# One written list for the attention phase of a windowed-attention and expert-layer kernel

## The chip, the cores and the metric

The kernel runs on one core of a Trainium2 chip. The metric is device time in microseconds (us) of one execution. The engines are named as in the profile: PE (TensorE) multiplies matrices, PEld is its weight load, DVE (VectorE), ACT (ScalarE) and POOL (GpSimd) do the work on elements, SP issues the DMAs. Each engine takes its own instructions strictly in the order in which the program lists them, and waits at the first one whose inputs or buffers are not ready.

## The reference

Three layers in a row, in float32: a causal attention with a window of 64 keys, four ReLU experts weighted by gate probabilities, and a layer with x·cos(x).

```python
scores = scale * np.matmul(q, k.transpose(0, 1, 3, 2))     # 2 batches, 8 heads, 576 rows, 64 wide
scores = np.where((rel >= 0) & (rel < 64), scores, -1e9)
attn = np.exp(scores - scores.max(-1)) ; attn = attn / (attn.sum(-1) + 1e-09)
x = np.matmul(attn, v)                                     # then 1152 rows of 512
p = domain_probs / (domain_probs.sum(-1) + 1e-09)
for e in range(4):
    out += p[:, e:e + 1] * (np.maximum(x @ w1[e], 0.0) @ w2[e])
h = out @ w_in
return (h * np.cos(h)) @ w_out
```

## The kernel before, in words

**Precision.** A float32 product is made of three fast products: each operand is split into a high part and a low part, and high·high, high·low and low·high are summed. Each weight unit (128 x 1024 numbers) is therefore loaded as `raw`, then split: ACT writes `whi` (`split_hi`, L160), POOL subtracts and writes `wlo` (`split_lo`, L168, in two halves for the first 16 units; unit 4 goes to DVE). The activations have `xhi` and `xlo`, the hidden layer `hh` (ACT) and `hl` (DVE).

**Attention** works on 18 blocks of 64 query rows. A block u goes through stages, named by letters in the code: R (POOL or ACT turns q, L219), S (PE scores, for a pair of blocks, L300), M (DVE mask and row maximum, two instructions, L315), E (ACT four exponentials and a row sum, L328), N (DVE reciprocal, then POOL multiplies, L341), T (PE transposes, L348), P (DVE copies, L355), V (PE times v, for a pair, L360) and X (ACT writes `xhi`, DVE `xlo`, for a pair, L377). PE therefore needs results of DVE, ACT, POOL and DVE again between S and V of one pair.

**Experts.** The 1152 rows are cut into three groups: 256 rows (blocks 0 to 3), 384 (blocks 4 to 9) and 512 (blocks 10 to 17). An expert's hidden layer is cut in halves; group g of half-expert e has four A steps (`emit_a`, L456: 12 matmuls into one bank of PSUM, then `hh` and `hl`) and four B steps (`emit_b`, L513, which sums into 2, 3 or 4 banks). Half-experts 0 and 1 run over the three groups first, so that the first group's experts can start while the attention of later blocks still runs. A step of the first group needs `xhi` and `xlo` of blocks 0 to 3, and units 0 to 3 (for e = 0) or 4 to 7 (e = 1).

**What sets the order.** A short list `START` (L616) fixes the order up to the first A step. After that each stage has a due time (`WHEN`, L596), and `between` (L664), which is called after every three matmuls of a step, issues what is due. Weight units are loaded and split by a pace (`weights`, L680, with a few early exceptions in `EARLY`), at the end of steps. `hh`, `hl` and an expert's weighted sums (`finish`, L552) are issued at once when their matmuls have been issued. Small matmuls on a constant (`keep_busy`, L285) fill PE's gaps in START.

**Shared buffers.** Four PSUM banks serve scores, transposes, V's results and the A steps in turn (`bank`, L71); four `raw` buffers serve the weight loads; SP issues all loads in one queue.

Of the kernel before, what the change touches and what calls it, by code (L numbers as in the profile page):

```python
# [24 lines left out]
def tile_window_attention_moe_cosglu(  # L25
# [134 lines left out]
    def split_hi(n):  # L160
        hi = wp.tile(list(raw_t[n].shape), F32R, tag="whi", name="whi")
        nc.scalar.activation(out=hi, in_=raw_t[n], func=AF.Copy)  # L162
        w_hi[units[n]] = hi
# [16 lines left out]
    LO_DVE = (4,)  # L180
    LO_HALF = 16

    EARLY = {3: 1, 4: 4, 5: 0, 6: 2, 7: 9}

    def split_unit(n):
        split_hi(n)
        if n in LO_DVE:
            split_lo(n, nc.vector)
        elif n < LO_HALF:
            split_lo(n, nc.gpsimd, 0)  # L190
            later(0.5, split_lo, n, nc.gpsimd, 1)
        else:
            split_lo(n, nc.gpsimd)
# [106 lines left out]
    def att_s(u):  # L300
        if u % 2:
            return
# [38 lines left out]
    def att_n(u):  # L341
        e, r = e_t.pop(u), sm_t.pop(u)
        ri = smp.tile([P, NP, 1], F32, tag="ri", name="ri")
        nc.vector.reciprocal(out=ri[:, :, 0], in_=r)
        nc.gpsimd.tensor_tensor(out=e, in0=e, in1=ri.to_broadcast([P, NP, 2 * W]), op=ALU.mult)  # L345
        pn_t[u] = e
# [108 lines left out]

    def emit_a(s):  # L456
# [3 lines left out]
        whi, wlo = w_hi[e, 0, u], w_lo[e, 0, u]  # L460
        xh, xl = xhi[g], xlo[g]
        assert all(("X", j | 1) in done for j in range(G0[g] // W, (G0[g] + n) // W))
        ps = bank("ph")[:, :n]
        cs = slice(P * fo, P * (fo + 1))
        for d in range(KD):
            nc.tensor.matmul(out=ps, lhsT=whi[:, d, cs], rhs=xh[:, d, :], start=d == 0, stop=False)  # L466
            nc.tensor.matmul(out=ps, lhsT=whi[:, d, cs], rhs=xl[:, d, :], start=False, stop=False)  # L467
            nc.tensor.matmul(  # L468
                out=ps, lhsT=wlo[:, d, cs], rhs=xh[:, d, :], start=False, stop=d == KD - 1
            )  # L470
            between((d + 1) / KD)
        hh = hp.tile([P, 512], F32R, tag="hh", name="hh")[:, :n]
        hl = hp.tile([P, 512], F32R, tag="hl", name="hl")[:, :n]
        if e < NM:
            nc.scalar.activation(out=hh, in_=ps, func=AF.Relu)  # L475
            nc.vector.scalar_tensor_tensor(  # L476
                out=hl, in0=ps, scalar=0.0, in1=hh.bitcast(F32), op0=ALU.max, op1=ALU.subtract
            )
            h_t[s] = (hh, hl)
        else:  # L480
            cos_stages(s, ps, hh, hl, n)

# [30 lines left out]
    def emit_b(s):  # L513
# [3 lines left out]
        whi, wlo = w_hi[e, 1, u], w_lo[e, 1, u]  # L517
        hh, hl = h_t.pop(s)
        first, last = f == 0, f == NFC - 1
        no = n // P  # L520
        if first:
            b_ps[g] = [psb.tile([P, 512], F32, tag="psb", name="pb_acc") for _ in range(no)]
        for i in range(no):
            ps = b_ps[g][i]
            cs = slice(P * i, P * (i + 1))
            ops = ((hh[:, cs], whi[:, fo, :]), (hh[:, cs], wlo[:, fo, :]), (hl[:, cs], whi[:, fo, :]))
# [24 lines left out]

    def finish(e, g):  # L552
        n = GS[g]
        pss = b_ps.pop(g)
        if e < NM:
# [5 lines left out]
            for i in range(n // P):  # L561
# [3 lines left out]
                if e == 0:  # L565
                    nc.vector.tensor_scalar(out=a, in0=pss[i], scalar1=p, scalar2=None, op0=ALU.mult)
                    continue
                nc.vector.scalar_tensor_tensor(  # L568
                    out=a, in0=pss[i], scalar=p, in1=a, op0=ALU.mult, op1=ALU.add
                )  # L570
# [20 lines left out]
    stage = {  # L591
        "S": att_s, "M": att_m, "E": att_e, "N": att_n, "T": att_t, "P": att_p, "V": att_v,
        "X": att_x, "R": att_r,
    }

    WHEN = dict(zip("SMENTPVX", (0.0, 0.21, 1.07, 1.09, 1.94, 2.07, 2.55, 2.73)))  # L596
    DEPTH = 3.1
    done = set()

    def att(what, j, *args):  # L600
        if 0 <= j < NB and (what, j) not in done:
            done.add((what, j))
# [12 lines left out]

    START = (  # L616
# [3 lines left out]
    )  # L620
    loads = {"q": load_q, "k": load_k, "v": load_v, "u": load_unit, "D": load_unit}
# [3 lines left out]
    for x in START.split():  # L625
        what, j = x[0], int(x[1:] or 0)
        if what in loads:
            loads[what](j)
        elif what == "g":
            load_gate()  # L630
        elif what == "Y":
            gate_t()
        elif what == "G":
            gate()
        elif what == "H":
            split_hi(j)
        elif what == "L":
            split_lo(j, nc.gpsimd, 0)
        elif what == "l":
            split_lo(j, nc.gpsimd, 1)  # L640
        elif what == "W":
            keep_busy(j)
        elif what.islower():
            att(what.upper(), j, nc.scalar.copy)
        else:
            att(what, j)
    make_mask((1,))
    R0 = GS[0] // W
    flat = sorted(
        (r - R0 + at, what, r)  # L650
        for r in range(R0, NB) for what, at in (*WHEN.items(), ("R", -0.9 - r % 2))
        if (what, r) not in done
    )
    pos = [0]


    def side_upto(x):
        while pos[0] < len(flat) and flat[pos[0]][0] <= x:
            att(*flat[pos[0]][1:])
            pos[0] += 1  # L660

    X0, X1, X2 = -1.0, GS[1] // W + DEPTH - 0.3, NB - R0 + DEPTH

    def between(part):  # L664
# [15 lines left out]
    def weights(t):  # L680
        n = nsplit[0]
        if t < EARLY.get(n, paced[0] + PACE):
# [13 lines left out]
    T1, T2 = SPL * TV - 2, 2 * SPL * TV - 2  # L696
# [9 lines left out]
    for t, (what, s) in enumerate(seq):  # L706
# [10 lines left out]
        if t == T2:  # L717
            side_upto(X2)
            assert pos[0] == len(flat)
# [44 lines left out]
```

## Time and profile before

| | |
|---|---|
| median of 3 runs | 661.45 us (661.2 to 662.39) |
| the profiled execution | 661.49 us |
| its span in the trace | 659.7 us |
| PE busy | 645.8 us, 98% |
| DVE, ACT, POOL busy | 377.5, 272.8, 152.4 us |
| mean granted clock of TensorE | 0.995 |

The profile is of one execution. Its first two parts say how long each engine was busy and in which fortieth of the span; the chain of work says what the last instruction waited for, step by step. A busy PE is not PE at its peak: its matmuls overlap and at a lower granted clock each takes longer. So the useful views here are those of a stretch: its windows (busy time and clock), and the instructions in order of time with the idle time ahead of each.

### The profile page before, as it was taken

How to read it: one execution, taken by the hardware profiler on the slowest of the kernel's cores; microseconds unless marked ns; L12 is line 12 of the kernel's file. 1: busy time of each engine (PE TensorE's matmuls, PEld its weight loads, DVE VectorE, ACT ScalarE, POOL GpSimd, SP SyncE). 2: the span in 40 equal slices, each digit the busy share in tenths (PEclk: the TensorE clock that was granted, in tenths of full speed). 3: DMA queues.
4: the chain of work that ended last, by engine and by line, in shares of the span. 5: the costliest groups of instructions: out<-in, count | busy, mean ns of one | idle time of the engine just before them, and what ended most of it. 6: DMA issues, size and time to landing. Idle time of an engine off the chain costs nothing.

```text
span 659.7 us, 9438 instructions
## 1 busy us (share of the span) xinstructions
PE 645.8 (98%) x3766; PEld 560.0 (85%) x3766; DVE 377.5 (57%) x563; ACT 272.8 (41%) x578; POOL 152.4 (23%) x117
## 2 busy tenths in 40 slices
PE   7889999999999999999999999999999999999997
PEld 6778888888899888899888899888988899988896
DVE  4466642174679566579665668834434355443554
ACT  6656531122123121113121112126876868865664
POOL 4864310231334021113121114012102202200000
PEclk9989999999999999999999999999999999999999
DMA  9565205105324621334342134231102100000022
GB/s 287 201 201 161 65 1 192 33 0 192 142 78 172 215 93 67 127 129 154 134 159 92 68 128 160 88 103 40 58 0 65 64 1 1 1 0 1 0 65 80
DMA packets 34686, 63.02 MB, mean 96 GB/s; under 512 B 2249, under 2 KB 18121, under 8 KB 34642
## 3 DMA queue, kind: packets, MB, share of 16 engines
q1 hardware_dynamic: 34642, 62.42, 28.0%
q8 instruction: 29, 0.48, 0.3%
q14 instruction: 15, 0.12, 0.1%
HBM read 51.66 MB, written 10.75 MB: 95 GB/s over the span
## 4 chain that ended last, share of the span: by engine, by line
PE 93%; POOL 2%; ACT 2%; DVE 1%; DMA 1%; issue 0%; SPq 0%; DVEq 0%; POOLq 0%; ACTq 0%
PE pb_acc L528 44%; PE ph L466 15%; PE ph L468 15%; PE ph L467 15%; PE psv L369 1%; POOL wlo L175 1%; PE pss L309 1%; PE pst L352 1%; POOL e L345 1%; PE psx L540 1%; DMA qraw<-in_q_dram 1%; ACT e L333 0%; PE idle_ps L287 0%; DVE nm L325 0%; ACT whi L162 0%
## 5 line engine op out<-in xcount | busy, mean ns | idle before, releaser
L175 POOL TENSOR_TENSOR wlo<-raw,whi 128x1024 fp32r<-128x1024 f32 (+1 forms) x62 | 121.6, 1972 | 372.9 <-ACT whi L162 283.6
L466 PE MATMUL ph<-xhi,whi 128*128 128x256 f32 (+2 forms) x576 | 195.4, 339 | 0.0
L467 PE MATMUL ph<-xlo,whi 128*128 128x256 f32 (+2 forms) x576 | 193.8, 336 | 0.1
L468 PE MATMUL ph<-xhi,wlo 128*128 128x256 f32 (+2 forms) x576 | 193.8, 336 | 0.0
L528 PE MATMUL pb_acc<-whi,hh 128*128 128x512 f32 x432 | 170.7, 395 | 0.3 <-ACT hh L502 0.3
L528 PE MATMUL pb_acc<-wlo,hh 128*128 128x512 f32 x432 | 169.8, 393 | 0.0
L528 PE MATMUL pb_acc<-whi,hl 128*128 128x512 f32 x432 | 169.3, 392 | 0.0
L475 ACT ACTIVATE hh<-ph 128x256 fp32r<-128x256 f32 (+2 forms) x96 | 47.0, 491 | 286.0 <-PE ph L468 283.0
L476 DVE SCALAR_TENSOR_TENSOR hl<-ph,hh 128x256 fp32r<-128x256 f32 (+2 forms) x96 | 52.9, 554 | 128.3 <-ACT hh L475 128.2
L466 PEld LDWEIGHTS ph<-xhi,whi 128*128 128x128 f32 x576 | 109.1, 189 | 10.9 <-issue 0.5
L467 PEld LDWEIGHTS ph<-xlo,whi 128*128 128x128 f32 x576 | 109.1, 189 | 10.3 <-DVE xlo L387 0.3
L468 PEld LDWEIGHTS ph<-xhi,wlo 128*128 128x128 f32 x576 | 109.0, 189 | 7.5
L528 PEld LDWEIGHTS pb_acc<-whi,hl 128*128 128x128 f32 x432 | 81.5, 189 | 17.6 <-DVE hl L505 0.2
L528 PEld LDWEIGHTS pb_acc<-whi,hh 128*128 128x128 f32 x432 | 81.8, 189 | 16.4 <-issue 0.8
L528 PEld LDWEIGHTS pb_acc<-wlo,hh 128*128 128x128 f32 x432 | 81.7, 189 | 14.4
L490 DVE SCALAR_TENSOR_TENSOR r<-kk,ph 128x256 f32<-128x256 f32 (+2 forms) x48 | 26.6, 555 | 64.5 <-ACT kk L489 64.5
L162 ACT ACTIVATE whi<-raw 128x1024 fp32r<-128x1024 f32 x48 | 50.6, 1054 | 2.1 <-DMA raw<-in_moe_w_dram 2.1
L488 ACT ACTIVATE kk<-ph,bias_m 128x256 f32<-128x256 f32 (+2 forms) x48 | 27.9, 581 | 39.5 <-PE ph L468 39.3
L568 DVE SCALAR_TENSOR_TENSOR acc<-pb_acc,gate_p,acc 128x512 f32<-128x512 f32 x63 | 43.2, 741 | 0.0
L499 DVE TENSOR_TENSOR ph<-ph,r 128x256 f32<-128x256 f32 (+2 forms) x48 | 27.0, 562 | 27.6 <-ACT r L496 27.6
L505 DVE TENSOR_TENSOR hl<-ph,hh 128x256 fp32r<-128x256 f32 (+2 forms) x48 | 26.6, 555 | 16.7 <-ACT hh L502 16.7
L333 ACT ACTIVATE e<-s,nm 128x128 f32<-128x128 f32 x72 | 27.9, 390 | 13.5 <-DVE nm L325 13.5
(65 smaller groups left out, 484.6 us busy)
## 6 DMA issues: line engine op xcount, KB each, us to landing
raw<-in_moe_w_dram SPq DMA_DIRECT2D x32, 512.0 KB, 6.1
raw<-in_moe_w_in_dram SPq DMA_DIRECT2D x8, 1024.0 KB, 6.9
w<-r SPq DMA_DIRECT2D x16, 512.0 KB, 3.1
raw<-in_moe_w_out_dram SPq DMA_DIRECT2D x8, 1024.0 KB, 6.9
raw<-w SPq DMA_DIRECT2D x16, 512.0 KB, 4.0
vr<-in_v_dram SPq DMA_DIRECT2D x16, 256.0 KB, 4.1
qraw<-in_q_dram SPq DMA_DIRECT2D x18, 128.0 KB, 4.4
out_dram<-acc SPq DMA_DIRECT2D x18, 128.0 KB, 1.8
```

Source lines behind the costliest of these rows:

```text
L162: nc.scalar.activation(out=hi, in_=raw_t[n], func=AF.Copy)
L175: engine.tensor_tensor(out=lo[:, cs], in0=t[:, cs], in1=hi[:, cs], op=ALU.subtract)
L333: nc.scalar.activation(out=e[:, p], in_=s[:, p], func=AF.Exp, bias=nm[:, p:p + 1], scale=1.0, accum_out=sm[:, p:p + 1],)
L466: nc.tensor.matmul(out=ps, lhsT=whi[:, d, cs], rhs=xh[:, d, :], start=d == 0, stop=False)
L467: nc.tensor.matmul(out=ps, lhsT=whi[:, d, cs], rhs=xl[:, d, :], start=False, stop=False)
L468: nc.tensor.matmul(out=ps, lhsT=wlo[:, d, cs], rhs=xh[:, d, :], start=False, stop=d == KD - 1)
L475: nc.scalar.activation(out=hh, in_=ps, func=AF.Relu)
L476: nc.vector.scalar_tensor_tensor(out=hl, in0=ps, scalar=0.0, in1=hh.bitcast(F32), op0=ALU.max, op1=ALU.subtract)
L488: nc.scalar.activation(out=kk, in_=ps, func=AF.Identity, bias=bias_m, scale=1.0 / TWO_PI)
L499: nc.vector.tensor_tensor(out=ps, in0=ps, in1=r1, op=ALU.mult)
L528: nc.tensor.matmul(out=ps, lhsT=a, rhs=b, start=first and m == 0, stop=last and m == 2)
L568: nc.vector.scalar_tensor_tensor(out=a, in0=pss[i], scalar=p, in1=a, op0=ALU.mult, op1=ALU.add)
```

## The change

The list `START`, the due times `WHEN` and the early exceptions `EARLY` go. One list, `ORDER`, names everything up to the end of the attention: loads (q, k, v, u), attention stages, splits of weight units 0 to 7 (H and J for `whi` on ACT and DVE, L and l for the halves of `wlo` on POOL, D for `wlo` on DVE), and, as h, j and f, the experts' `hh`, `hl` and sums, each with a place of its own. A point in the list ends a piece: three matmuls of an A step or one block of rows of a B step. `piece` runs the list up to the next point, ahead of the three matmuls. N is parted into I (the reciprocal on DVE) and N (POOL), X into x (ACT) and X (DVE). `whi` of unit 0 moves from ACT to DVE, and DVE makes `wlo` of unit 2 in the place of unit 4. Units 8 to 15 are split on POOL by one instruction each, not two halves. 33 small filler matmuls stand in the place of 27. After the list's end the kernel runs as before.

```diff
-    def split_hi(n):
+    def split_hi(n, copy=nc.scalar.copy):
...
-    EARLY = {3: 1, 4: 4, 5: 0, 6: 2, 7: 9}
...
-    def att_n(u):
-        e, r = e_t.pop(u), sm_t.pop(u)
+    def att_i(u):
+        r = sm_t.pop(u)
...
+    def side(kind, fn, *args):
+        if script:
+            queues[kind].append((fn, args))
+        else:
+            fn(*args)
+
+    def piece():
+        while script:
+            x = script.pop(0)
+            if x == ".":
+                break
+            token(x)
...
         for d in range(KD):
+            piece()
+            if d == 0:
+                whi, wlo = w_hi[e, 0, u], w_lo[e, 0, u]
+                xh, xl = xhi[g], xlo[g]
+                ps = bank("ph")[:, :n]
...
-            nc.scalar.activation(out=hh, in_=ps, func=AF.Relu)
-            nc.vector.scalar_tensor_tensor(
-                out=hl, in0=ps, scalar=0.0, in1=hh.bitcast(F32), op0=ALU.max, op1=ALU.subtract
-            )
-            h_t[s] = (hh, hl)
+            side("h", relu_high, ps, hh)
+            side("j", relu_low, s, ps, hh, hl)
...
-    WHEN = dict(zip("SMENTPVX", (0.0, 0.21, 1.07, 1.09, 1.94, 2.07, 2.55, 2.73)))
...
-        "k0 q0 q1 q2 q3 v0 v1 u0 W9 R0 r1 S0 W2 k1 v2 v3 g R2 r3 S2 u1 u2 u3 W8 M0 M1 E0 N0 M2 E1 "
...
+        q0 q1 k0 q2 q3 u0 v0 R0 v1 r1 q4 q5 k1 W10 S0 v2 R2 g R3 u1 M0 C0 u2 q6 q7 M1 W5 S2 E0 v3 u3
...
+        H2 T5 L1 v6 S6 x3 v7 P5 H3 q12 X3 R9 V5 k3 M6 l1 H4 q13 . v8 . x5 L3 M7 . u5 E6 . v9 .. L4
...
+        "J": lambda n: split_hi(n, nc.vector.tensor_copy),
+        "D": lambda n: split_lo(n, nc.vector),
...
-    nload, nsplit = [5], [3]
+    nload, nsplit = [8], [8]
...
-        if t < EARLY.get(n, paced[0] + PACE):
+        if script or t < paced[0] + PACE:
             return
```

**Ahead of the first A step, on PE.** Before, T3 (pst), V3 (psv) and S4 (pss) stand ahead of the first three matmuls of A (ph); idle_ps are the fillers.

```order
L352 MATMUL pst<-ident,e 128x128 x4
L287 MATMUL idle_ps<-idle 128x128 x2
L369 MATMUL psv<-pt,vr 64x64 x16
L309 MATMUL pss<-kT,qt 64x128 x16
L466 MATMUL ph<-xhi,whi 128x256
L467 MATMUL ph<-xlo,whi 128x256
L468 MATMUL ph<-xhi,wlo 128x256
```

The same place now, from T4 on:

```order
L345 MATMUL pst<-ident,e 128x128 x4
L276 MATMUL idle_ps<-idle 128x128 x2
L360 MATMUL psv<-pt,vr 64x64 x16
L345 MATMUL pst<-ident,e 128x128 x4
L296 MATMUL pss<-kT,qt 64x128 x16
L360 MATMUL psv<-pt,vr 64x64 x16
L482 MATMUL ph<-xhi,whi 128x256
```

T4, V3, T5, S6 and V5 now stand ahead of the first A step: S6, T4, T5 and V5 have moved there from places between the steps.

**POOL around the first two steps of blocks 4 and up.** Before, with buffer numbers: e is N's product (blocks 4 to 8 in this order), wlo_512, 645 and 699 are units 3, 5 and 6.

```order
L175 TENSOR_TENSOR wlo_512<-raw_238,whi_510 128x512 x2
L345 TENSOR_TENSOR e_444<-e_444,ri_530 128x512
L345 TENSOR_TENSOR e_591<-e_591,ri_599 128x512
L345 TENSOR_TENSOR e_628<-e_628,ri_636 128x512
L222 COPY qt_639<-qraw_434 128x64x4
L222 COPY qt_641<-qraw_436 128x64x4
L175 TENSOR_TENSOR wlo_645<-raw_514,whi_643 128x512 x2
L175 TENSOR_TENSOR wlo_699<-raw_613,whi_697 128x512 x2
L345 TENSOR_TENSOR e_736<-e_736,ri_746 128x512
```

The same stretch now: wlo_577 and 611 are units 3 and 4, 723 and 745 units 5 and 6; e_588, 622, 737 and 762 are blocks 6 to 9.

```order
L175 TENSOR_TENSOR wlo_577<-raw_267,whi_529 128x512
L175 TENSOR_TENSOR wlo_611<-raw_428,whi_561 128x512 x2
L175 TENSOR_TENSOR wlo_577<-raw_267,whi_529 128x512
L338 TENSOR_TENSOR e_588<-e_588,ri_630 128x512
L338 TENSOR_TENSOR e_622<-e_622,ri_657 128x512
L175 TENSOR_TENSOR wlo_723<-raw_586,whi_676 128x512
L175 TENSOR_TENSOR wlo_745<-raw_650,whi_721 128x512
L175 TENSOR_TENSOR wlo_723<-raw_586,whi_676 128x512
L338 TENSOR_TENSOR e_737<-e_737,ri_770 128x512
```

N4 and N5 are long past here, four halves of splits stand ahead of N6, and three between N7 and N8.

**ACT over the first A steps, now.** whi_561, 676 and 721 are units 4, 5 and 6; e_588 and e_622 are E6 and E7, hh the results of A steps.

```order
L162 CAST whi_561<-raw_428 128x1024
L375 CAST xhi_574<-psv_536 128x4x128
L320 ACTIVATE e_588,sm_589<-s_556,nm_558 128x128 x4
L325 ACTIVATE r_594<-sm_589,bias_e_100 128x4
L320 ACTIVATE e_622,sm_623<-s_579,nm_581 128x128 x4
L325 ACTIVATE r_628<-sm_623,bias_e_100 128x4
L497 ACTIVATE hh_599<-ph_565 128x256
L497 ACTIVATE hh_620<-ph_604 128x256
L497 ACTIVATE hh_647<-ph_632 128x256
L162 CAST whi_676<-raw_586 128x1024
L497 ACTIVATE hh_673<-ph_652 128x256
L162 CAST whi_721<-raw_650 128x1024
```

Three weight splits, each of which waits for its load, now stand ahead of E6, of the fourth hh and of E8 (the next row), and E6 and E7 ahead of the first hh; before, one split stood among the first four hh, with E4 ahead of them and E5 behind.

## Rows read from the trace of the kernel before

**Rows 1.** The page, part 1: busy us, share, instructions of each engine.
```profile
PE 645.8 (98%) x3766; PEld 560.0 (85%) x3766; DVE 377.5 (57%) x563; ACT 272.8 (41%) x578; POOL 152.4 (23%) x117
```

**Rows 2.** Windows: stretch, length, busy PE, PEld, DVE, ACT, POOL; clock, DMA share, GB/s.
```profile
21.41:105.59 84.18, 78.78 (x771) 67.83 (x767) 48.03 (x90) 42.63 (x155) 35.69 (x43) 0.96 0.40 125
105.59:659.70 554.11, 549.52 (x2767) 476.75 (x2765) 319.11 (x446) 216.34 (x379) 103.94 (x48) 1.00 0.24 84
```

**Rows 3.** PE in time: start, us, engine, line, what [idle before, releaser].
```profile
21.41 0.39 PE L466 MATMUL ph<-xhi,whi 128*128 128x256 f32 x1
...
27.58 0.40 PE L528 MATMUL pb_acc<-whi,hh 128*128 128x512 f32 x1
...
31.10 0.66 PE L352 MATMUL pst<-ident,e 128*128 128x128 f32 x4 [2.66 <-POOL e L345]
...
46.07 1.12 PE L352 MATMUL pst<-ident,e 128*128 128x128 f32 x4 [2.40 <-POOL e L345]
```

**Rows 4.** DVE in time: the reciprocals that release N4 and N7.
```profile
26.17 0.17 DVE L344 RECIPROCAL ri<-r 128x4 f32<-128x4 f32 x1
...
43.23 0.18 DVE L344 RECIPROCAL ri<-r 128x4 f32<-128x4 f32 x1 [1.48 <-ACT r L338]
```

**Rows 5.** POOL in time: the splits ahead of N4 and of N7.
```profile
27.55 2.50 POOL L175 TENSOR_TENSOR wlo<-raw,whi 128x512 fp32r<-128x512 f32 x2
...
40.02 5.00 POOL L175 TENSOR_TENSOR wlo<-raw,whi 128x512 fp32r<-128x512 f32 x4
```

**Rows 6.** Windows: the two stretches of half clock.
```profile
32.33:35.73 3.40, 3.40 (x26) 2.53 (x15) 2.44 (x6) 0.18 (x1) 1.04 (x1) 0.50 0.34 89
...
45.98:49.39 3.41, 3.32 (x13) 2.86 (x13) 2.13 (x5) 1.61 (x8) 1.28 (x3) 0.50 0.04 15
```

**Rows 7.** Chain of work: start, us, what; a T, an S and a V at full clock.
```profile
64.18 0.44 PE pst L352 x4
...
69.83 1.03 PE pss L309 x32
...
77.08 1.08 PE psv L369 x32
```

**Rows 8.** ACT in time: the first exponentials of blocks 0 and 1.
```profile
8.89 0.40 ACT L333 ACTIVATE e<-s,nm 128x128 f32<-128x128 f32 x1 [1.59 <-DVE nm L325]
...
10.78 0.38 ACT L333 ACTIVATE e<-s,nm 128x128 f32<-128x128 f32 x1
```

**Rows 9.** Groups: line, engine, what, count; busy us, mean ns, idle before (DVE, ACT to 110 us).
```profile
L325 DVE TENSOR_REDUCE nm<-s 128x4 f32<-128x512 f32 x18 | 12.4, 686 | 0.6
L320 DVE SCALAR_TENSOR_TENSOR s<-pss,mask 128x512 f32<-128x512 f32 x18 | 12.1, 671 | 6.6 <-PE pss L309 6.2 <-PE ph L468 0.3
L357 DVE COPY pt<-pst 128x512 f32<-128x512 f32 x17 | 11.6, 684 | 10.1 <-PE pst L352 10.0
...
L175 DVE TENSOR_TENSOR wlo<-raw,whi 128x1024 fp32r<-128x1024 f32 x1 | 1.4, 1385 | 0.0
...
L345 POOL TENSOR_TENSOR e<-e,ri 128x512 f32<-128x512 f32 x18 | 18.7, 1042 | 39.9 <-DVE ri L344 38.6 <-DMA kT<-in_k_dram 1.4
...
L162 ACT ACTIVATE whi<-raw 128x1024 fp32r<-128x1024 f32 x8 | 8.4, 1053 | 0.0
...
L386 ACT CAST xhi<-psv 128x512 fp32r<-128x512 f32 x9 | 5.3, 588 | 9.7 <-PE psv L369 9.7
```

**Rows 10.** SP in time: k1's load; then loads' time to landing, of kT and raw.
```profile
7.10 0.42 SPq L238 DMA_DIRECT2D kT<-in_k_dram  x1
...
DMA to landing us min/median/max: 4.0/5.6/6.1
...
DMA to landing us min/median/max: 3.5/6.1/9.5
```

**Rows 11.** DVE and POOL in time, later: one instruction alone, and beside a POOL split.
```profile
141.74 1.23 DVE L140 SCALAR_TENSOR_TENSOR r<-raw,x 128x1024 f32<-128x1024 uint32 x1
...
165.89 3.67 POOL L175 TENSOR_TENSOR wlo<-raw,whi 128x512 fp32r<-128x512 f32 x2 [5.61 <-ACT whi L162]
...
166.22 2.19 DVE L140 SCALAR_TENSOR_TENSOR r<-raw,x 128x1024 f32<-128x1024 uint32 x1
```

More of the change, by code (lines that the diff above doesn't have):

```diff
@@ L178, in split_lo @@
             w_lo[units[n]] = half_lo.pop(n)
-    LO_DVE = (4,)
-    LO_HALF = 16
-    EARLY = {3: 1, 4: 4, 5: 0, 6: 2, 7: 9}
     def split_unit(n):
         split_hi(n)
[L187 to L193, printed above, removed]
+        split_lo(n, nc.gpsimd)
     actx = ExitStack()
@@ L454, in issue_upto @@
             fn(*args)
+    queues = {"h": [], "j": [], "f": []}
+    script = []
+    def side(kind, fn, *args):
[9 more added lines that the diff above has]
+            token(x)
+        if not script:
+            for kind in queues:
+                while queues[kind]:
+                    fn, args = queues[kind].pop(0)
+                    fn(*args)
     def emit_a(s):
@@ L516, in emit_b @@
         u, fo = divmod(f, 2)
-        whi, wlo = w_hi[e, 1, u], w_lo[e, 1, u]
-        hh, hl = h_t.pop(s)
+        hh = None
         first, last = f == 0, f == NFC - 1
         no = n // P
-        if first:
-            b_ps[g] = [psb.tile([P, 512], F32, tag="psb", name="pb_acc") for _ in range(no)]
         for i in range(no):
+            cs = slice(P * i, P * (i + 1))
+            piece()
+            if hh is None:
+                whi, wlo = w_hi[e, 1, u], w_lo[e, 1, u]
+                hh, hl = h_t.pop(s)
+                if first:
+                    b_ps[g] = [psb.tile([P, 512], F32, tag="psb", name="pb_acc") for _ in range(no)]
+            ops = ((hh[:, cs], whi[:, fo, :]), (hh[:, cs], wlo[:, fo, :]), (hl[:, cs], whi[:, fo, :]))
             ps = b_ps[g][i]
-            cs = slice(P * i, P * (i + 1))
-            ops = ((hh[:, cs], whi[:, fo, :]), (hh[:, cs], wlo[:, fo, :]), (hl[:, cs], whi[:, fo, :]))
             for m, (a, b) in enumerate(ops):
@@ L622, in tile_window_attention_moe_cosglu, with token @@
+    def token(x):
+        if x in queues:
+            fn, args = queues[x].pop(0)
+            fn(*args)
+        elif x in ("g", "Y0", "G0", "C0"):
+            calls[x[0]]()
+        else:
+            calls[x[0]](int(x[1:]))
     make_mask((0,))
@@ L624, in tile_window_attention_moe_cosglu @@
     make_mask(())
[L625 to L662, printed above, removed]
+    for x in ORDER.split():
+        script.extend(x if x[0] == "." else [x])
     def between(part):
@@ L717, in tile_window_attention_moe_cosglu @@
         if t == T2:
-            side_upto(X2)
-            assert pos[0] == len(flat)
+            assert not script
             actx.close()
```

94 lines of the change are left out of this document (46 added, 48 removed), and 2 rows, old and new, of the table START.

## The prediction, made before the changed kernel ran

> **What bounds the kernel now.** I read the busy times first. PE is busy 98% of the span [rows 1], so time can come only from what PE loses. The windows say where: from 105.59 us on, where the third group's experts begin, PE is busy 549.5 of 554.1 us at full clock, and the changed list has ended by then, so that part stays as it is. In the 84.2 us between the first A step (21.41) and 105.59 PE is idle for 5.4 us and its mean clock is 0.96 [rows 2]. Third, PE's instructions in order of time with the idle time ahead of each: almost all of these 5.4 us are two waits, 2.66 us ahead of T4 at 31.10 and 2.40 us ahead of T7 at 46.07, and both end with POOL's product N [rows 3]. Fourth, why N was late. The reciprocal for N4 was done at 26.3, but POOL began two halves of a weight split at 27.55 and kept at them until 30.05; the one for N7 was done at 43.4, while POOL was in four halves from 40.02 to 45.02 [rows 4, 5]. So POOL's order, not its load (23% busy), held PE. Last, the clock: after each of the two waits, and nowhere else in this stretch, PE is granted 0.50 (1.2 of 2.4 GHz) for 3.4 us [rows 6].
>
> **What the two waits cost.** Idle: 2.66 + 2.40 = 5.06. The two half-clock stretches do half of what they would at full clock: (3.40 + 3.41) / 2 = 3.4. Together 8.5 us, and the most that the middle of the change can win.
>
> **What the change does to them.** At T4's old place nothing is left to wait for: T4 and T5 now stand ahead of the first A step, T6 and T7 behind the first B step. I follow the list with durations from rows. A split's half on POOL takes 1.25 (2.50 for two [rows 5]), an N 1.04, a P 0.68, an M 0.67 + 0.69, a split of whi on ACT 1.05, an xhi 0.59 [rows 9]; an E takes 1.89 from one to the next [rows 8]; on PE an S 1.03, a T 0.44, a V 1.08 [rows 7], four A steps 6.2 (21.41 to 27.58 [rows 3]).
>
> **Start of the first A step.** It now stands behind V5, not V3. The loads of q0 and q1 go ahead of k0, which I take as 0.4 us earlier for the first scores (0 to 0.8, an estimate), so E0 begins at 8.5, not 8.89 [rows 8]. On ACT five E follow each other, to 8.5 + 5 x 1.89 = 17.9; xhi of blocks 0 and 1 comes behind V1 at about 18.7, E5 ends at 20.6, its reciprocal at 20.9. N5 waits on POOL behind two copies of q: between 20.9 and 22.0, I take 21.5, so it ends at 22.5. T5 ends at 23.1, S6 at 24.1; P5 runs beside S6, and V5 ends at 25.2, where the first A step begins. That is 25.2 against 21.41: **+3.8 us** (2.8 to 5.3). Of the moved work, S6 + T4 + T5 + V5 = 1.03 + 0.88 + 1.08 = **3.0 us** no longer stand between the steps. So the later start is nearly paid for by PE work that is done in it; net +0.8.
>
> Two things are hidden here. S4 now stands ahead of T0 and waits for k1: issued at 7.10 or a little sooner, landing at most 6.1 us later [rows 10], 13.2. Then M4 ends at 15.6, and E4's place on ACT comes at 16.1. That covers 0.5 us of lateness; beyond it k1 delays everything one to one. And the whi of unit 0 on DVE (no row shows a copy of that size there) stands between M3 and M4, while S4 waits anyway; bounds 0.5 to 1.39 (a P is 0.68 for half as much from PSUM, the subtraction of that size 1.385 [rows 9]), I take 1.0, since both lie in DVE's wait for S4.
>
> What is not hidden: between the fillers behind S2 and S4 PE stands idle for about 3 us, as long as the two waits of rows 3. I expect a stretch of half clock there too. It costs at most 1.7; only T0, T1 and V1 lie on the chain to E5, so I take **+0.5** (0 to 1.7).
>
> **New waits behind it.** ACT takes the whi of units 4, 5 and 6 in list order, each behind its load, with E6, E7 and the first hh behind unit 4, and E8 behind unit 6. Unit 4 can be issued when POOL is done with unit 0 and SP is past v5, at 19.0; with the median landing of 6.1 [rows 10] its whi ends at 26.2, xhi 26.8, E6 and E7 30.6, the first two hl at 31.9. S8 takes the banks of the first two A steps, so it waits until 31.9; PE is there at 25.2 + 5.9 = 31.1 (the four steps without the late start of the first): 0.8. T6 and T7 then come at 34: N6 and N7 end at 32 and 33 although four halves of splits stand ahead of them on POOL, so they wait for nothing. V7 needs P7, which stands on DVE behind the fourth hl (34.2: its hh is behind unit 5, 26.2 + 6.1 + 1.05), M8, M9 and P6: 34.2 + 2 x 1.36 + 2 x 0.68 = 38.3 against PE at 37.6: 0.7. T8 needs E8, which is behind unit 6 (about 30.5 + 6.1 + 1.05 = 37.6): E8 39.5, N8 40.8, against 40.5 on PE: 0.3. T9 takes the bank of an A step whose hl comes behind E9, unit 7 and xhi, at 44.5, against 43.5: 1.0. Sum 2.8, none of them half as long as the two of rows 3, so I count no half clock here. Of these, lateness that PE collects itself takes some away (each change from one kind of matmul to another costs PE a little, in both kernels); bounds 0 and 5, I take **+1.5**. From there to the third group (S10 to S16, T10 to T17) every N, P and bank is ready by the same count when PE comes. hl and the sums on DVE get places behind M and P; PE reads an hl at the earliest two steps later, so that costs nothing while DVE keeps its list, and shows up in T9 if not.
>
> **The rest** costs nothing: POOL's subtraction in one piece for units 8 to 15 takes the same 2.5 us, and POOL is idle there; I, x and N as separate tokens are the same instructions; six more fillers stand in idle time; loads of units 8 and 9 move to the end of the list, some 25 us ahead of their splits.
>
> **A rule against the change.** A DVE instruction with two inputs takes 1.23 us alone and 2.19 where a POOL split runs beside it, and that pair of halves takes 3.67, not the 2.50 of rows 5 [rows 11, 5]. The change puts two such neighbours together: whi of unit 0 on DVE beside N1, and wlo of unit 2 on DVE amid POOL's four halves. The Trainium skill, SBUF — State Buffer, section "Who interferes with whom", says that DVE and GpSimd share one pair of ports as an exclusive lock, held for the whole instruction, for DVE copies in a two-port mode and DVE instructions with two SBUF inputs. The trace agrees. By that rule the subtraction of unit 2 would end up to 1.25 us later and S8 would wait that much longer, which is a sum of up to 657.1; without it, 655.8. Much of it would only shorten the wait ahead of V7, so I leave the sum.
>
> **The sum**, against the profiled execution's 661.5 (the median is 661.45, so the same): 661.5 - 8.5 + 3.8 - 3.0 + 0.5 + 1.5 = **655.8 us**.
>
> **The rivals.**
> A: *nothing new is late.* The four waits of 2.8 us vanish, since loads land sooner than the median, and no half clock falls into the start: 661.5 - 8.5 + 0.8 = 653.8, with the start 1 us sooner 652.8. For it: landings go down to 3.5 us [rows 10]. Against: four separate chains on ACT would all have to come early.
> B: *the waits only move.* Chains of ACT and DVE take the place of POOL's: the waits at S8, V7, T8 and T9 reach 5 us, one of them grows as long as those of rows 3 and a half-clock stretch (1.7) follows: 661.5 - 8.5 + 0.8 + 0.5 + 5 + 1.7 = 661.0. For it: hh was never behind an E of later blocks or a load before, and is now. Against: each wait is about 1 us by the count.
> C, *slower: loads hold ACT.* ACT is in order, and two loads decide: unit 4 ahead of E6, E7 and all hh of the first steps, and unit 6 ahead of E8 and E9. With more loads in flight (units 1 and 2 are now ahead of q6, q7 and k2) a landing may take the longest in the rows, 9.5 us in place of 6.1. Each lateness goes to S8 or T8 one to one: 3.4 us at unit 4, some 2 at unit 6, and both waits then are as long as those of rows 3, so two half-clock stretches come back, 3.4. 655.8 + 3.4 + 2.0 + 3.4 = 664.6. With both stretches back it is slower than before from 2.3 us of lateness on, and measurably so from 3.6. Against: DMA is lightly used from 21 us on (0.40 of its time [rows 2]), when unit 6 is loaded.
>
> **How the numbers follow.** Forecast 0.67, A 0.15, B 0.10, C 0.08. A measurement of this kernel can tell about 0.2%, 1.3 us, from no change: faster is under 660.1, slower over 662.8. The forecast's own bounds: 652.8 with everything at its good end; at the other, start 25.2 + 1.5, waits of 3 and the half clock at 1.0, it is 659.3. The range goes from A's better part to just short of B: 651.8 to 660.5. Faster: forecast, A and a little of B, 0.83; same, most of B, 0.09; slower, C and the rest of B, 0.08.
>
> **What would show it.** The first A step at 25.2 (24 to 27), with V5 right ahead of it. No wait of PE over 1.2 us behind it, none that ends with N at T6 or T7; small ones ahead of S8, V7, T8, T9 that end with hl, P or N. No stretch of half clock between 26 and 105, perhaps one between 12 and 18. The first 512-wide A step at about 100, not 105.59, and the same length of everything behind it. The forecast is wrong if PE waits over 2 us for DVE or ACT behind a weight split, if E5 ends well past 20.6, or if the length behind the third group's start changes by more than 1 us.

## The result, and the profile of the changed kernel

The changed kernel takes 654.71 us (median of four runs, 653.16 to 656.21) against 661.63 for the kernel before on the same chip: a ratio of 0.989, 95% interval 0.986 to 0.993. Run again later it took 653.62 us against 660.89, ratio 0.989 (0.987 to 0.990). The prediction was 655.8 us, in a range of 651.8 to 660.5. The profiled execution took 653.36 us, with a span of 651.6 us.

First the page's part 1, then the windows (stretch, length, then busy us of PE, PEld, DVE, ACT, POOL, the granted clock, DMA share, GB/s): two around S4's wait, then the stretch from the first A step to the third group's first A step, and from there to the end. The last two answer to [rows 1, 2].

```profile
PE 642.8 (99%) x3778; PEld 559.0 (86%) x3778; DVE 378.2 (58%) x564; ACT 269.8 (41%) x576; POOL 150.3 (23%) x110
```

```profile
9.05:12.78 3.73, 1.61 (x17) 1.45 (x13) 3.66 (x8) 3.67 (x20) 1.81 (x3) 1.00 1.09 345
12.78:17.00 4.22, 4.22 (x58) 3.74 (x60) 3.65 (x7) 4.15 (x23) 4.22 (x5) 1.00 1.07 374
...
25.24:97.14 71.90, 71.33 (x699) 62.68 (x695) 42.55 (x80) 35.65 (x135) 30.81 (x31) 1.00 0.47 150
97.14:651.60 554.46, 549.50 (x2767) 476.71 (x2765) 319.32 (x446) 215.86 (x379) 100.26 (x40) 1.00 0.24 81
```

The stretch is 71.90 us long, where it was 84.18. PE is idle in it for 0.57 us, not 5.4, and its clock is 1.00, not 0.96. What lies behind it has kept its length (554.46 against 554.11). The same three lengths in a sum: start 25.24 - 21.41 = +3.83, stretch 71.90 - 84.18 = -12.28, behind +0.35; together -8.10, which is the difference of the spans.

PE in order of time (start, us, engine, line, what; in brackets idle time ahead and what ended it): S4, the last work ahead of the first A step, that step, and then every place where a wait was forecast.

```profile
12.78 1.10 PE L296 MATMUL pss<-kT,qt 64*64 64x128 f32 x32 [2.12 <-DMA kT<-in_k_dram]
...
24.16 1.15 PE L360 MATMUL psv<-pt,vr 128*64 128x64 f32 x32
25.24 0.38 PE L482 MATMUL ph<-xhi,whi 128*128 128x256 f32 x1
...
31.17 1.38 PE L296 MATMUL pss<-kT,qt 64*64 64x128 f32 x32
...
33.98 0.60 PE L345 MATMUL pst<-ident,e 128*128 128x128 f32 x4
...
34.82 0.63 PE L345 MATMUL pst<-ident,e 128*128 128x128 f32 x4 [0.25 <-DVE hl L500]
...
38.56 1.15 PE L360 MATMUL psv<-pt,vr 128*64 128x64 f32 x30 [0.27 <-DVE pt L350]
...
40.79 0.60 PE L345 MATMUL pst<-ident,e 128*128 128x128 f32 x4
...
43.36 0.60 PE L345 MATMUL pst<-ident,e 128*128 128x128 f32 x4
```

V5 stands right ahead of the first A step. S8 (31.17) takes 0.28 us more from its start to the next work than an undisturbed S (1.31 against the 1.03 of [rows 7]), T6 and T7 (33.98) 0.35 more than two T by [rows 7] (1.23 from 33.98 to 35.21, against 0.88), V7 0.59 more (1.67 from 37.97 to 39.64, against 1.08). T8 (40.79) and T9 (43.36) wait for nothing. Nowhere does PE wait for N, which ended both waits of [rows 3].

ACT and DVE tell where the small waits come from. ACT in order of time, then DVE:

```profile
29.98 0.91 ACT L497 ACTIVATE hh<-ph 128x256 fp32r<-128x256 f32 x3
32.89 1.05 ACT L162 CAST whi<-raw 128x1024 fp32r<-128x1024 f32 x1 [1.99 <-DMA raw<-in_moe_w_dram]
33.84 0.38 ACT L497 ACTIVATE hh<-ph 128x256 fp32r<-128x256 f32 x1
```

```profile
28.53 2.15 DVE L175 TENSOR_TENSOR wlo<-raw,whi 128x1024 fp32r<-128x1024 f32 x1
...
34.25 0.42 DVE L500 SCALAR_TENSOR_TENSOR hl<-ph,hh 128x256 fp32r<-128x256 f32 x1 [2.51 <-ACT hh L497]
```

ACT stands for 1.99 us at the split of unit 5, whose load, issued at 25.97, landed 6.9 us later; the fourth hh is queued behind it, its hl starts on DVE at 34.25, and behind that hl are M8, M9 and P7, for which V7 waits. The chain is the forecast one, link by link.

The chain of work that ended last (start, us, what) shows which load held the start:

```profile
2.11 3.79 DMA qraw<-in_q_dram
...
7.00 5.64 DMA kT<-in_k_dram
...
25.97 6.89 DMA raw<-in_moe_w_dram
```

The middle one is k1, for which S4 waits at 12.78, the last one unit 5.

### The profile page after: what moved, and what is told of

Same layout as the page of the kernel before. It is cut to its first block, busy times and chain, and to the rows that moved or that the text cites. A ratio compares the mean times of both kernels' runs of the same rounds, so it can differ in the third digit from the quotient of the medians.

```text
span 651.6 us, 9445 instructions
## 1 busy us (share of the span) xinstructions
PE 642.8 (99%) x3778; PEld 559.0 (86%) x3778; DVE 378.2 (58%) x564; ACT 269.8 (41%) x576; POOL 150.3 (23%) x110
## 4 chain that ended last, share of the span: by engine, by line
PE 94%; DMA 3%; DVE 2%; ACT 1%; POOL 0%; SPq 0%; issue 0%; DVEq 0%
PE pb_acc L553 44%; PE ph L482 15%; PE ph L484 15%; PE ph L483 15%; PE psv L360 1%; PE pst L345 1%; DMA raw<-in_moe_w_dram 1%; PE pss L296 1%; DMA kT<-in_k_dram 1%; PE psx L565 1%; DMA qraw<-in_q_dram 1%; DVE nm L312 0%; DVE pt L350 0%; POOL e L338 0%; DVE s L307 0%
## 5 line engine op out<-in xcount | busy, mean ns | idle before, releaser
L175 POOL TENSOR_TENSOR wlo<-raw,whi 128x1024 fp32r<-128x1024 f32 (+1 forms) x54 | 119.0, 2210 | 383.0 <-ACT whi L162 292.6
L162 ACT CAST whi<-raw 128x1024 fp32r<-128x1024 f32 x47 | 48.9, 1044 | 4.6 <-DMA raw<-in_moe_w_dram 4.6
```

The source lines that it names most:

```text
L162: copy(out=hi, in_=raw_t[n])
L175: engine.tensor_tensor(out=lo[:, cs], in0=t[:, cs], in1=hi[:, cs], op=ALU.subtract)
```

## Experiments

Times are medians; "again" is the changed kernel's second set, 653.62 us, the measure for the rest. Each ratio is against the kernel before in the same set. The sets ran on four chips, on which the kernel before took 660.89 us (up to h0_on_act), 661.36 (up to a_sooner), 660.95 (up to d2_pool) and 661.16 (the last run), so a difference of half a us between sets can be that of the chips.

**The changed kernel once more.**

> The changed kernel as it is, again. Its four runs fell into two pairs, 653.2 and 653.4, and 656.1 and 656.2, and the second pair has a lower mean clock (0.998 and 0.996 against 0.999 and 1.000). Theory 1: the second pair has a stretch of half clock (3.4 us) that begins in or behind PE's 2.1 us wait ahead of S4; then runs at 656 show a mean clock at least 0.002 lower than runs at 653, each time, and nothing lies between the pairs. Theory 2: k1 lands later in some runs; then times spread between 653 and 656 with one clock.

Measured: 652.78 to 653.97 us in four runs. In the first set two runs had lain at 653.2 and 653.4 and two at 656.1 and 656.2; the pair at 656 did not come back. Its mean clocks were 0.998 and 0.996, against 0.999 and 1.000 for the pair at 653, but neither of the two was traced, so its cause stays open. The first A step of this trace starts at 24.99, S4's wait is 1.52 us, the third group's first A step comes at 96.5. Landings differ by some tenths from run to run, and the start with them.

**Fillers in the idle time ahead of S4**, to see whether a half clock hides there.

```diff
- R4 k2 M2 R5 q8 E1 q9 I0 M3 N0 W6 S4 E2 I1
+ R4 k2 M2 R5 q8 E1 q9 I0 M3 N0 W14 S4 E2 I1
```

> Edit: 14 fillers, not 6, ahead of S4, so that PE does not stand idle while it waits for k1. Theory 1 (half clock behind that wait makes the 656 runs): all runs near 653.3, the median 1 to 1.5 us under that of the changed kernel. Theory 2 (late landing of k1): two kinds of runs as before, medians equal within 0.5. Rival: the clock falls somewhere else; same two kinds. The profiled run itself should show S4 at 12.8 as before and no time gained if it is of the fast kind.

Measured: 654.65 us (652.89 to 656.12), ratio 0.990 (0.989 to 0.992): no gain. The windows of the changed kernel above say why: PE is idle for 2.12 us ahead of 12.78, and the clock stays at 1.00 in both windows. In the profiled execution there was nothing to mend. One run of this set, again without a trace, took 656.12 at a mean clock of 0.997, so the fillers did not do away with such runs. The profiled execution here is 1.3 us longer than the changed kernel's for another reason. k1 landed later and the first A step starts at 25.64, 0.4 later; and the load of unit 5 landed at 34.2, so that in PE's order of time T7 waits for the hl behind it:

```profile
36.13 0.63 PE L345 MATMUL pst<-ident,e 128*128 128x128 f32 x4 [1.15 <-DVE hl L500]
```

**Only POOL's order, in the kernel before.** The halves of units 3, 5 and 6 are put off behind N4 and N7; all else stays.

```diff
+    LATE_LO = {3: 2.2, 5: 2.5, 6: 2.6}
...
+        elif n in LATE_LO:
+            later(LATE_LO[n], split_lo, n, nc.gpsimd, 0)
+            later(LATE_LO[n] + 0.5, split_lo, n, nc.gpsimd, 1)
```

> Edit on the kernel before, and nothing of the new list: the halves of the subtraction of units 3, 5 and 6 on POOL are put off by 2.2 to 2.6 steps, so that N4 stands ahead of unit 3 and N7 ahead of units 5 and 6. Theory (POOL's order made the two waits of 2.66 and 2.40 us and the two stretches of half clock): PE waits for N at T4 and T7 fall under 1 us each, both stretches of half clock go, 653.5 to 657. At T7 some 0.9 may stay, since the row sum of block 7 was only done at 43.1. Rival (the gain of the change is in the start or in hh, hl and sums having own places): under 2 us gained, waits move to the subtractions that come later.

Measured: 659.50 us (658.37 to 661.83) against 660.89, ratio 0.998 (0.997 to 0.999). PE and POOL in order of time, and the window behind the last wait:

```profile
28.60 0.66 PE L356 MATMUL pst<-ident,e 128*128 128x128 f32 x4 [0.21 <-POOL e L349]
...
41.42 0.66 PE L356 MATMUL pst<-ident,e 128*128 128x128 f32 x4 [0.91 <-POOL e L349]
...
52.56 1.11 PE L356 MATMUL pst<-ident,e 128*128 128x128 f32 x4 [2.79 <-POOL e L349]
```

```profile
46.50 5.01 POOL L175 TENSOR_TENSOR wlo<-raw,whi 128x512 fp32r<-128x512 f32 x4
51.44 1.06 POOL L349 TENSOR_TENSOR e<-e,ri 128x512 f32<-128x512 f32 x1
```

```profile
52.58:55.99 3.41, 3.41 (x13) 2.83 (x13) 2.25 (x5) 0.38 (x1) 2.51 (x3) 0.50 0.29 102
```

The two waits of [rows 3] fall from 2.66 and 2.40 to 0.21 and 0.91, and both stretches of half clock are gone, so POOL's order was the cause of these waits. But four halves now stand at 46.50, ahead of N9, and T9 waits 2.79 us for it; 3.41 us of half clock follow. Only 1.4 us come out, so the 653.5 to 657 expected were missed. A due time can move a split, but where it lands is again ahead of some N. In a list each place can be chosen by itself. How much a better set of due times could have won wasn't tried.

**The whi of unit 0 back on ACT.**

```diff
- S4 E2 I1 T0 J0 Y0 M4
+ S4 E2 I1 T0 H0 Y0 M4
```

> Edit: whi of unit 0 is made by ACT again, at the same place of the list (between E1 and E2 there), not by DVE. Theory (the chain of E0 to E5 on ACT sets the first A step, and DVE had time while it waited for S4): E2 to E5 and with them the first A step come 1.05 us later, at 26.3, and the end 0.8 to 1.1 us later. Rival (DVE's or POOL's list sets the start): no change, within 0.3 us, or a gain, since DVE gets 1.2 us back.

Measured: 654.32 us (653.63 to 654.73), ratio 0.990 (0.989 to 0.992). PE in order of time:

```profile
20.54 0.66 PE L345 MATMUL pst<-ident,e 128*128 128x128 f32 x4 [0.68 <-POOL e L338]
26.35 0.39 PE L482 MATMUL ph<-xhi,whi 128*128 128x256 f32 x1
```

The first A step starts 1.1 to 1.4 us later, about the 1.05 that a split takes in ACT's chain of exponentials; T3 ahead of it now waits 0.68 us for its N. The end is only 0.7 us later: unit 5's load is then relatively sooner, T6 and T7 wait for nothing and V7 for some 0.3.

**The split of unit 5 behind the fourth hh.**

```diff
- h j . h l3 j . j H5 S8 N6 u7 h . j k4
+ h j . h l3 j . j S8 N6 u7 h H5 . j k4
```

> Edit: on ACT the whi of unit 5, which waits for its load until about 33, moves behind the fourth hh, which it held until 33.8. Theory (what is left of waits, and the slower pair of runs, come from loads of units that hold ACT: the fourth hl frees T7's bank and stands ahead of M8, M9, P6 and P7, so T7 and V7 wait for the load of unit 5): PE's wait at T6 and T7 (0.37) goes, V7's extra 0.6 falls, the end comes 0.5 to 1.0 sooner than the changed kernel's 653.4, and no run is over 655. Rival (the slower runs are something else): the fast runs gain the same, but about one run in four stays some 2.5 us over the others.

Measured: 652.97 us (652.30 to 655.39), ratio 0.989 (0.987 to 0.991). PE in order of time, and a window of the stretch:

```profile
34.54 1.03 PE L345 MATMUL pst<-ident,e 128*128 128x128 f32 x8
37.95 1.15 PE L360 MATMUL psv<-pt,vr 128*64 128x64 f32 x32
```

```profile
26.00:100.00 74.00, 74.00 (x709) 65.25 (x709) 42.52 (x79) 36.13 (x136) 30.75 (x31) 1.00 0.44 145
```

The waits at T7 and V7 are gone, and PE has no idle time at all in these 74 us, although unit 5 landed still later than in the changed kernel (issued at 26.42, landed 7.2 us later). The stretch from the first A step to the third group's takes 70.84 us, against 71.90 and 71.56 in the two traces of the changed kernel. But the first A step came at 25.80 here, so the gain in the time is 0.6 us and lies within what landings and chips do. One run was at 655.39 at full clock; its cause stays open.

**The split of unit 5 ahead of the first hh.**

```diff
- l4 u6 . h I7 . h j . h l3 j . j H5 S8
+ l4 u6 . H5 h I7 . h j . h l3 j . j S8
```

> Edit, the other way: the whi of unit 5 moves ahead of the first three hh, so that all four stand behind its load. Theory (ACT is in order, a load's lateness goes to PE one to one): the first hh comes at 33.9 and not 30.0, the first two hl at 35, S8 waits for its bank until then (PE idle 3 to 3.5 us behind 31.2), a stretch of half clock follows (1.7), and the end comes 2.5 to 5 us later, 656 to 658. Rival (the banks and hl have slack): under 1 us later.

Measured: 658.18 us (654.66 to 660.46), ratio 0.996 (0.994 to 0.998). ACT, then PE in order of time, then windows:

```profile
32.28 1.04 ACT L162 CAST whi<-raw 128x1024 fp32r<-128x1024 f32 x1 [2.41 <-DMA raw<-in_moe_w_dram]
33.23 1.20 ACT L497 ACTIVATE hh<-ph 128x256 fp32r<-128x256 f32 x4
```

```profile
34.13 2.30 PE L296 MATMUL pss<-kT,qt 64*64 64x128 f32 x32 [3.09 <-DVE hl L500]
```

```profile
33.81:37.20 3.39, 3.07 (x34) 2.61 (x35) 2.27 (x6) 1.56 (x4) 2.77 (x3) 0.50 0.30 111
37.20:40.64 3.44, 3.44 (x14) 2.85 (x13) 2.11 (x4) 2.96 (x15) 0.75 (x1) 0.50 0.54 152
```

One token moved by a few places, and rival C stands there: ACT waits 2.41 us for a load, all four hh are queued behind it, S8 waits 3.09 us for a bank, and there are 6.8 us at 1.2 GHz, in which PE is busy for 6.5, which cost another 3.3. Over half of the change's gain is lost. The shortest run, 654.66, had a mean clock of 1.000, the longest, 660.46, of 0.992, so much of the loss seems to go with the clock; only the profiled execution was traced.

**A half of unit 5's subtraction ahead of N6.**

```diff
- H5 S8 N6 u7 h . j k4 . N7 M8 T6 H6 L5
+ H5 S8 L5 N6 u7 h . j k4 . N7 M8 T6 H6
```

> Edit: on POOL one half of the subtraction of unit 5 stands ahead of N6, where it stood behind N7; it waits for whi of unit 5 (33.9). Theory (in the kernel before, one or more halves ahead of N made PE's two waits and the half clock): N6 ends at 36.2, not 32.8, so T6 waits 2.0 to 2.4 us at 34 and T7 up to 1 more; with the waits that this takes from V7 the end comes 2 us later without and 3.5 with a stretch of half clock, 655.5 to 657. Rival (PE finds other work): under 0.5 us later.

Measured: 655.21 us (654.98 to 657.28), ratio 0.992 (0.990 to 0.994). PE in order of time:

```profile
36.44 0.66 PE L345 MATMUL pst<-ident,e 128*128 128x128 f32 x4 [1.95 <-POOL e L338]
```

POOL, in order, waits at the half for ACT's split and with it for the load; N6 is behind. The wait of the kernel before is back, smaller. V7's own wait is gone in return, so the end is 1.6 us later.

**The first A step sooner**, with T5, S6 and V5 behind the first matmuls again, and x3, X3 ahead of the splits.

```diff
- N5 H1 q11 W2 V3 R8
- H2 T5 L1 v6 S6 x3 v7 P5 H3 q12 X3 R9 V5 k3 M6 l1 H4 q13 . v8 . x5 L3 M7 . u5 E6 . v9 .. L4
+ N5 q11 W2 V3 x3 X3 H1
+ R8 H2 L1 v6 H3 q12 R9 l1 H4 q13 . T5 v7 P5 . S6 k3 M6 . V5 v8 . x5 L3 M7 u5 E6 . v9 . L4
```

> Edit: T5, S6 and V5 go back behind the first three matmuls of A each, as the kernel before had such work between its steps, and xhi and xlo of blocks 2 and 3 stand ahead of the splits on ACT. Theory (the later start is paid for by work that fills PE's wait for those blocks): the first A step starts at about 24.0, 1.2 sooner, but PE is idle ahead of it for the 1.4 us that T5, S6 and part of V5 filled, and the end comes 0.5 to 1.5 us later than the changed kernel's. Rival (the +3.8 us of the start is a loss that could be had back): the end comes 0.5 to 1.2 us sooner.

Measured: 655.51 us (654.71 to 655.78), ratio 0.991 (0.990 to 0.993). PE in order of time:

```profile
23.38 0.39 PE L482 MATMUL ph<-xhi,whi 128*128 128x256 f32 x1 [0.69 <-ACT xhi L375]
...
33.24 1.42 PE L296 MATMUL pss<-kT,qt 64*64 64x128 f32 x32 [0.31 <-DVE hl L500]
```

The step starts 1.6 to 1.9 us sooner and the whole ends 1.9 us later, more than the 0.5 to 1.5 expected: S8, which followed 5.93 us behind the first A step in the changed kernel, follows 9.86 behind here. The work between has only moved, and PE lost time beside it: it waits 0.69 us ahead of the step, 0.34 in it and 0.31 at S8, and changes more often from one kind of matmul to another (57 pieces of like matmuls in the stretch, against 51).

**The load of k0 first again**, alone, and together with the split of unit 5 behind the fourth hh.

```diff
- q0 q1 k0 q2 q3 u0
+ k0 q0 q1 q2 q3 u0
```

> One part undone: the load of k0 goes ahead of those of q0 and q1 again, as in the kernel before. Theory of the prediction's start: the change of that order is worth about 0.4 us (0 to 0.8), because q0's copy on POOL or ACT ends last ahead of the first scores. With it undone the first scores should begin at about 6.0 us, not at 5.67 or sooner, the first A step 0.3 to 0.5 us later (25.3 to 25.7 against 25.0 to 25.2), and the median 0.2 to 0.4 us above the changed kernel's 653.6. Rival: the scores of block 4, which wait 2.1 us for k1, take the difference up; then the first A step and the time stay where they are, within 0.2 us.

> Two edits at once: the whi of unit 5 behind the fourth hh (as in the run h5_late, 652.97 us) and the load of k0 first again. If the two are independent, the waits at T6, T7 and V7 are gone as in h5_late and the start is as in the run k0_first, so the time is h5_late's plus what k0 first costs there: 653.0 to 653.4 by the theory, 653.0 by the rival that k1 takes it up. A start under 25.2 us here would speak for loads that happen to land differently, not for the order of these two.

Measured: 653.99 us (653.36 to 655.91) alone, ratio 0.990 (0.988 to 0.991), and 652.59 us (652.33 to 652.71) together, ratio 0.987 (0.985 to 0.989), the shortest time of all. The medians are +0.4 and -0.4 against the kernels with q0 first, so they don't agree on a sign. PE in order of time in the first of the two:

```profile
5.90 1.35 PE L296 MATMUL pss<-kT,qt 64*64 64x128 f32 x32 [0.24 <-POOL qt L211]
13.93 1.10 PE L296 MATMUL pss<-kT,qt 64*64 64x128 f32 x32 [2.80 <-DMA kT<-in_k_dram]
...
26.39 0.39 PE L482 MATMUL ph<-xhi,whi 128*128 128x256 f32 x1
```

The first scores start at 5.90, against 5.67 and 5.92 in two executions of the changed kernel. What sets the first A step is k1: it lands at 13.80 here, at 12.64 and 12.39 in those two, 13.12 in the run of both edits, and in all four traces the first A step starts 12.46 or 12.47 us behind S4. It is issued behind two loads of q that wait for a buffer, and its time of issue went from 6.97 to 8.04 under either order (8.03 with q0 first, in the run with the later split). That speaks for the rival, that earlier first scores are lost in the wait for k1. But the 0.4 us that the prediction gave to this edit can't be told from the spread of landings in the times; the experiment doesn't settle it.

**The subtraction of unit 2 back on POOL**, alone and on top of the run of both edits (the three points are points of the list).

```diff
- E7 I6 . D2 ... l4 u6
+ E7 I6 . L2 ... l2 l4 u6
```

> One part undone: the subtraction of unit 2 goes back to POOL in two halves at the same place of the list, and DVE is free of it. In the changed kernel it takes 2.15 us on DVE (1.385 alone) beside five halves on POOL that take 7.28 (6.3 alone). Theory (the two lengthen each other while they overlap): the seven halves on POOL now take their undisturbed 1.25 to 1.27 each, 8.8 us in all, so POOL ends them at 33.4 instead of 31.8, 1.6 us later and not 2.5; the product of block 7 ends at 35.4, T6 and T7 at 34 wait 0.8 to 1.5 us in all, the first hl is done at the same time or up to 1 us sooner, and the end moves by +0.3 to +1.2 us (653.9 to 654.8). Rival (no lengthening by the neighbour; the halves are slow for another reason): seven halves take 10.2 us, N6 and N7 end 2.9 us later than now, T6 and T7 wait over 2 us, and a stretch of half clock may follow; 656 or more.

> The kernel of the run h5_late_k0 (652.59 us), with the subtraction of unit 2 on POOL in two halves, as in d2_pool. In d2_pool PE was 0.97 us behind the changed kernel after the second B step (the products of blocks 6 and 7 end later on POOL), but 0.65 of it came back since the wait ahead of V7 was gone, and S8's 0.28 as well, so the time stayed. Theory (a loss costs nothing while it lies ahead of another wait that would have ended later): here V7 waits for nothing, so the loss behind POOL shows: T6 at a gap of 0.5 to 0.8 us, PE 0.5 to 0.9 later at V7 than without the edit, and 653.1 to 653.5 in the median. Rival (the subtraction on DVE is no better than on POOL at all, because DVE's hl come sooner): 652.3 to 652.7.

Measured: 653.05 us (652.66 to 654.48), ratio 0.988 (0.987 to 0.990) alone: under the forecast, and no loss against the 653.62. On top of the two edits 653.23 us (652.93 to 653.51), ratio 0.988 (0.986 to 0.989), against 652.59: 0.6 us slower, of which the chips can make 0.2. POOL in order of time in the changed kernel, the second line being the last of the five, read in a window of its own:

```profile
24.55 7.28 POOL L175 TENSOR_TENSOR wlo<-raw,whi 128x512 fp32r<-128x512 f32 x5
29.52 2.30 POOL L175 TENSOR_TENSOR wlo<-raw,whi 128x512 fp32r<-128x512 f32 x1
31.78 2.04 POOL L338 TENSOR_TENSOR e<-e,ri 128x512 f32<-128x512 f32 x2
```

and with the subtraction on POOL:

```profile
24.32 8.80 POOL L175 TENSOR_TENSOR wlo<-raw,whi 128x512 fp32r<-128x512 f32 x7
33.06 2.06 POOL L338 TENSOR_TENSOR e<-e,ri 128x512 f32<-128x512 f32 x2
```

The seven halves take 1.26 us each. Of the five, the first four take 1.24 from one to the next, and the one that began while DVE was in the subtraction of unit 2 (28.53 to 30.68) took 2.30. So two more halves cost POOL 1.5 us, not 2.5. N6 and N7 then end later, and PE waits 0.5 us at T6 and 0.3 at T7 in both runs with this edit. Alone it costs nothing, since S8 and V7 no longer wait (V7 takes 1.08 from start to end); PE comes to V9 0.2 us later than in the second set's trace (44.93, not 44.70). Where V7's wait had been taken away already, the loss stays: the stretch from the first A step to the third group's takes 71.79 us, against 70.73 without the edit; alone it takes 71.77, against 71.90 and 71.56. A loss is paid only if no later wait would have swallowed it.

## Why the prediction was right, and where a term was off

**What bounded the kernel: right.** The waits of [rows 3] and the half clock of [rows 6] are gone together, and the run with POOL's order alone changed shows that this order caused both waits. The term of -8.5 stands as a reading of the profiled execution. Its 3.4 us for the clock can't be had by themselves: in the sets of the experiments two runs of the kernel before had a mean clock of 1.000 and took 660.27 and 660.43 us, only 1.1 to 1.2 less than the profiled one with 0.995. They were not traced; it would fit if PE, coming sooner to the next wait for N, only waited longer there.

**Start of the first A step: right in the number, in part by luck.** 25.24 and 24.99 in two executions, 25.2 forecast, built from ACT's five exponentials in a row. By the trace the wait for k1 ended later: k1 landed at 12.64, and when ACT was through with the five, its xhi still waited 0.29 us for V1 on PE. In eight traces the first A step starts 12.46 or 12.47 us behind S4, whenever that comes (in h5_late and d2_pool_h5, where PE also waits 0.5 and 0.7 us for the gate's load behind S4, it is 13.0 and 13.2). So the 0.5 us of slack that the prediction gave to k1 was not there, and had k1 landed at the 13.2 that it allowed for, the start would have been near 25.8. The half clock expected ahead of S4 (+0.5) came in no trace; what the longer runs with a lower mean clock lost, and where, is not known. Of the parts, the later whi on ACT shows up one to one (h0_on_act); the 0.4 us for q0 ahead of k0 could not be shown.

**The moved work: right.** S6, T4, T5 and V5 lie ahead of the step, and the run that undoes most of it starts sooner and ends later.

**The new waits: places and causes half right, the sum by one missing term.** S8, T6 with T7 and V7 lose 0.28 + 0.35 + 0.59 = 1.22 us, where 1.5 was taken for S8, V7, T8 and T9. V7's chain is as written. T7's wait was not forecast; it ends with the same late fourth hl, which frees the bank that T7 takes. T8 and T9 were ready. But the stretch as a whole is -12.28, and -8.5 - 3.0 leave -0.8, not +1.5. What I left out is what the kernel before lost in small pieces there. The waits view of before shows it (waiting, for what: us in all, times, longest):

```profile
PE pst L352 <- POOL e L345: 7.2, 5, 2.7
```

Besides the two of 5.06 it waited for N three times more, twice ahead of 21 us and once for 0.28 at 55.70; an S at 60.11 took 0.32 too long (1.35 to the next work), and the four A steps from 21.41 took 0.23 longer than those of the changed kernel (6.17 against 5.94). That is 0.8. I worked out the rest by setting each piece of like matmuls against the time that so many take in a row: before had 65 such pieces from 21 to 105 us and after has 51 from 25 to 97, and in the parts without a wait each piece is some 0.06 to 0.07 longer than its matmuls. Fourteen fewer are 0.9 us, so 1.7 of the missing 2.0 have a name. The prediction named this cost and set it down as the same in both kernels, and it left out the third, smaller wait for N. That these 0.9 come from there is worked out, not shown by a run of its own, and the last 0.3 stay open.

The balance: -0.5 (no half clock), -2.3 (waits and pieces), +0.4 (behind the stretch) are -2.4, from 655.8 to 653.4, the profiled execution's time.

**The rivals.** A came out in the number: the profiled 653.36 and the second set's 653.62 lie between its 652.8 and 653.8, the first set's median of 654.71 between A and the forecast. Its reason holds in part. No trace has half clock at the start, and nothing is late at T8 and T9, since units 4 and 6 landed 5.5 and 4.9 us after their issue, sooner than the 6.1 taken; but 1.22 us of waits stayed, and what brought the time down was the small losses of the old order, which A doesn't name. B did not happen: the waits that ACT and DVE brought came to 1.22 us, not 5 (in before_pool the waits moved, but to another N on POOL). C did not happen, since neither load took the 9.5 us that it counts with, but its mechanism is real, as h5_early shows: ACT in order behind a load, lateness about one to one, half clock on top. Unit 5, the latest load here (6.9 us), did little harm because the list puts its split behind three of the four hh.

**The rule on the shared lock** (the Trainium skill, SBUF — State Buffer, section "Who interferes with whom") held: the subtraction of unit 2 took 2.15 us on DVE, where the like one alone took 1.385 [rows 9], and the one half on POOL that began beside it took 2.30, where the others took 1.24 to 1.26. By that rule the sum would have been up to 657.1; of the 0.77 us PE paid S8's 0.28, which is gone with the subtraction on POOL. For the rest no wait of PE is seen.

## What to carry to other kernels

When one in-order engine (here POOL) holds work that is urgent and work that is not, look at what stands ahead of the urgent instruction when its input is ready, and put the rest behind it; then check that it has not landed ahead of the next urgent one. On an in-order engine an instruction that waits for a load belongs behind everything that is ready, even at the price of its own lateness: moving one split by a few places was worth 5 us here. In the sum of a change, also count the small losses of the old order that go with it, and price an edit's loss only up to the next wait that would swallow it.

## What the runs showed of the hardware

- **Idle time and the clock.** After or at the end of waits of 2.66 and 2.40 us in the kernel before, 2.79 in before_pool and 3.09 in h5_early, PE was granted half clock, in stretches of 3.40, 3.41, 3.41 and 6.83 us. After 2.12 us in the changed kernel, 1.95 in pool_back, and 2.80 us ahead of S4 in k0_first, it was granted full clock. The length of one wait doesn't decide it alone; what does wasn't tried.
- **A float32 copy of 128 x 1024 on DVE** (whi of unit 0, both sides in SBUF) has two prices. DVE in order of time, in the first and in the second trace of the changed kernel:

```profile
12.32 1.23 DVE L162 CAST whi<-raw 128x1024 fp32r<-128x1024 f32 x1
```

```profile
12.67 0.66 DVE L162 CAST whi<-raw 128x1024 fp32r<-128x1024 f32 x1
```

  In the first it began 0.7 us before POOL ended N0 (13.00), in the second as N0 ended (12.70). N1, which POOL ran beside it, took 1.49 and 1.40, where N0 took 1.04. On ACT the same copy takes 1.05; the subtraction of that size on DVE, alone, took 1.385 [rows 9].
- **Landings.** The 512-KB load of unit 5, issued at 25.7 to 27.3 us, landed at 32.3 to 34.2 in the traces with nearly the same list ahead of it, and k1 at 12.4 to 13.8, with three to seven loads in flight. This spread of 1 to 2 us is of the size of the spread of the kernel's time; in the execution of fill_s4 the two late loads go with 0.4 us in the start and 0.9 in the stretch.
